# Placing units 5 to 8 of a retention layer by hand between the matmul blocks of the layer behind it

## The chip, the cores and the metric

The kernel runs on one core of one Trainium2 chip. The metric is the device time of one execution in microseconds; the median of 13 runs is compared. PE is the matrix engine (TensorE), ACT is ScalarE, DVE is VectorE, POOL is GpSimd and SP is SyncE, which only issues DMAs. Each engine has its own queue and works it off in the order in which the program wrote it. PSUM is the memory that PE writes its results into, SBUF the working memory.

## What is computed

A retention layer (attention without softmax, with a decay mask) of 8 batches, 8 heads, 576 positions and head size 64, and behind it a two-layer network on the 4608 tokens that come out:

```python
def _attn_ref(q, k, v):                       # q, k, v: (8, 8, 576, 64)
    scores = scale * np.matmul(q, k.transpose(0, 1, 3, 2))
    gamma = 1.0 - 2.0 ** (-5.0 - np.arange(H))
    Dmat = np.where(rel >= 0, gamma[:, None, None] ** rel[None, :, :], 0.0)
    return np.matmul(scores * Dmat[None], v)
...
x = attn_out.transpose(0, 2, 1, 3).reshape(B * S, H * D)    # (4608, 512)
h = x @ w_in                                                # (4608, 2048)
out = np.maximum(0.01 * h, h) @ w_out                       # (4608, 512)
```

## The kernel before

**Units.** The retention is cut into 40 units: each batch gives four of 128 positions and one of 64. Unit u goes through these helpers. `load` (L115) brings q, k and v of the unit into a ring of five buffers each (`ld`, L72), so the loads of unit u have to wait for the casts of unit u-5. `casts` (L169) makes float16 of them: k on ACT (L134), q and v with their decay tables on DVE, and from unit `NEARLY` = 11 on on POOL (L142, L162). `transposes` (L174) turns q and k on PE: four matmuls with an identity for k, ACT's copy of the result (L190), four for q, DVE's copy. From unit `NPE` = 9 on there is no PE transpose: `cast_q` issues a DMA transpose from SP instead (L150). `scores` (L196) makes the masked products inside two chunks of 64 (L204) and the unit's contribution to the running state (L214). `masks` (L221) multiplies with the triangle on DVE. `states` (L231) adds up the state on DVE, two or three instructions, and copies it to float16 (L252): on ACT below `NEARLY`, on POOL from there on. `outputs` (L294) multiplies the scores with v (L307) and the queries with the states before (L318), then ACT copies one half out of PSUM (L326) and DVE adds the other and writes `xT` (L330), the transposed input of the network.

**The network.** The tokens are cut into 18 groups of 256. `g1_blocks(g)` (L420) gives eight blocks of the first layer, each of eight matmuls (L432) and one leaky-relu on ACT (L439); they need `xT` of all units of the group and share two PSUM buffers (`hps`). `g2_blocks(g)` (L446) gives eight blocks of the second layer, each of four matmuls (L455), with a DVE copy (L465) and an output DMA from SP (L467) after the fourth and the eighth. For groups 0 and 1, `g2_wide` (L486) gives sixteen such blocks on four PSUM buffers, two of them `hps` (L500, L509, L511).

**The order.** The schedule is written out: the order of the calls is the order on every engine's queue (L82). The start (L521 to L568) is by hand. From L570 to L608 the wide blocks and those of `g1[2]` have units 5 to 8 put between them. From L609 on `run` (L475) interleaves the blocks of two groups and spreads steps over them. A step n is `steady(n)` (L378): the loads of unit n+6, `scores(n)`, `outputs(n-1)`, `casts(n+2)`, `masks(n)`, `states(n)`; the order inside depends on `NEARLY`. The steps begin with n = `NFIRST` = 7 (scores only; outputs from the next on). `NRING` = 12: loads up to unit 12 are issued from POOL at the start (L553 to L558), later ones from SP by the steps.

`tr` and `sc` are one PSUM tile for units 6 to 8 (`transposes(u, sc_pool)`, one buffer): their transposes, their scores and the states take turns in it.

Of the kernel before, what the change touches and what calls it, by code (L numbers as in the profile page):

```python
# [9 lines left out]
FP = mybir.dt.float32  # L10
# [7 lines left out]
def kernel(  # L18
# [22 lines left out]
    nc = tc.nc  # L41
    B, H, S, D = q.shape
    NT, DM = out.shape
    DFF = moe_w_in.shape[1]
    P = 128
# [3 lines left out]
    NF = DFF // P  # L49
# [48 lines left out]
    NU = len(units)  # L98
    nrows = [min(P, S - P * w) for b, w in units]
    NPE = 9  # L100
    NFIRST = 7
    NEARLY = 11
    NRING = 12
    t32 = {}
    qk16 = {}
# [1 line left out]
    qkT = {}  # L107
    s16s = {}
    st16 = {}
    carry = {}  # L110

    def half(i):
# [12 lines left out]
    def loads(u, eng):  # L125
        for x in (1, 0, 2):
            load(u, x, eng)
# [41 lines left out]
    def casts(u):  # L169
        cast_k(u)  # L170
        cast_q(u)
        cast_v(u)

    def transposes(u, pool=None):  # L174

        n = nrows[u]
        qkT[u] = b_pool.tile([P, 2, NP, P], F16, name="qkT")
        if pool is None:
            trs = [y_pool.tile([P, NP, P], F16, name="yps") for x in range(2)]
        else:  # L180
            both = pool.tile([P, 2, 2 * NP, P], F16, name="sc")
            trs = [both[:, x, 0:NP, :] for x in range(2)]
        for x in (1, 0):
            for p in range(NP):
                nc.tensor.transpose(  # L185
                    trs[x][:, p, 0:n],
                    qk16[u][0:n, x, 2 * p : 2 * p + 2, :].rearrange("t h d -> t (h d)"),
                    ident[0:n, 0:n],
                )
            (nc.scalar.copy if x else nc.vector.tensor_copy)(  # L190
                out=qkT[u][:, x, :, 0:n], in_=trs[x][:, :, 0:n]
            )
# [3 lines left out]
    def scores(u):  # L196

        nb = nrows[u] // CH
        a = sc_pool.tile([P, 2, 2, NP, CH], FP, name="sc")
        sc_tiles[u] = a  # L200
        for p in range(NP):
            for g in range(2):
                for j in range(nb):
                    nc.tensor.matmul(  # L204
                        out=a[half(j), g, 0, p, :],
                        lhsT=qkT[u][half(g), 1, p, half(j)],
                        rhs=qkT[u][half(g), 0, p, half(j)],
                        start=True, stop=True, skip_group_check=True,
                    )
        if nb == 2:  # L210
            for p in range(NP):
                for j in range(2):
                    for g in range(2):
                        nc.tensor.matmul(  # L214
                            out=a[half(g), j, 1, p, :],
                            lhsT=qk16[u][half(j), 1, 2 * p + g, :],
                            rhs=v16[u][half(j), 2 * p + g, :],
                            start=True, stop=True, skip_group_check=True,
                        )

    def masks(u):  # L221
        n = nrows[u]
        s16s[u] = a_pool.tile([P, 2, NP, CH], F16, name="s16")
        nc.vector.tensor_tensor(  # L224
            out=s16s[u][0:n],
            in0=sc_tiles[u][0:n, :, 0],
            in1=mask_sb[0:n].unsqueeze(1).unsqueeze(1).to_broadcast([n, 2, NP, CH]),
            op=MUL,
        )

    def states(u):  # L231
        b, w = units[u]
        if nrows[u] < P:
            return
        st = sc_tiles[u][:, :, 1]
        s32 = a_pool.tile([P, 2, NP, CH], FP, name="s32")
        if w == 0:
            nc.vector.tensor_copy(out=s32[:, 0], in_=st[:, 0])
        else:
            nc.vector.tensor_tensor(out=s32[:, 0], in0=st[:, 0], in1=carry[b], op=ADD)  # L240
        if w % 2 == 0:
            nc.vector.tensor_tensor(out=s32[:, 1], in0=st[:, 1], in1=s32[:, 0], op=ADD)  # L242
        else:
            tmp = a_pool.tile([P, NP, CH], FP, name="stmp")
            nc.vector.tensor_tensor(out=tmp, in0=st[:, 1], in1=s32[:, 0], op=ADD)
            nc.vector.tensor_tensor(
                out=s32[:, 1], in0=tmp,
                in1=gblk_sb.unsqueeze(2).to_broadcast([P, NP, CH]), op=MUL,
            )
        carry[b] = s32[:, 1]  # L250
        st16[u] = a_pool.tile([P, 2, NP, CH], F16, name="st16")
        (nc.scalar.copy if u < NEARLY else nc.gpsimd.tensor_copy)(out=st16[u], in_=s32)  # L252

    def st_before(u, j):
        if j:
# [38 lines left out]
    def outputs(u):  # L294


        n = nrows[u]
        nb = n // CH
        b, w = units[u]
        ot = ot_pool.tile([P, 2, 2 * NP, CH], FP, name="ot")  # L300
        own = ot[:, :, 0:NP]
        far = ot[:, :, NP : 2 * NP].rearrange("q r (s j) t -> q r s (j t)", j=2)
        for hp in range(NP):
            for h in (hp, hp + NP):
                o, c = divmod(h, NP)
                for j in range(nb):
                    nc.tensor.matmul(  # L307
                        out=own[half(o), j, c, :],
                        lhsT=v16[u][half(j), h, :],
                        rhs=s16s[u][half(j), h % 2, h // 2, :],  # L310
                        start=True, stop=True, skip_group_check=True,
                    )
        for j in range(nb):
            for s in range(2):
                for o in range(2):
                    for g in range(2):
                        p = 2 * o + s
                        nc.tensor.matmul(  # L318
                            out=far[half(o), g, s, half(j)],
                            lhsT=st_before(u, j)[half(g), p, :],  # L320
                            rhs=qkT[u][half(g), 0, p, half(j)],
                            start=True, stop=True, skip_group_check=True,
                        )
        t0 = (b * S + P * w) % XR
        tmp = a_pool.tile([P, NP, P], FP, name="own")
        nc.scalar.copy(  # L326
            out=tmp[:, :, 0:n].rearrange("q c (j t) -> q c j t", t=CH),
            in_=own[:, 0:nb].rearrange("q j c t -> q c j t"),
        )
        nc.vector.tensor_tensor(  # L330
            out=xT[:, :, t0 : t0 + n].rearrange("q (s g) t -> q g s t", g=2),
            in0=far[:, :, :, 0:n],
            in1=tmp[:, :, 0:n].rearrange("q (s g) t -> q g s t", g=2),
            op=ADD,
        )
# [41 lines left out]

    def steady(n):  # L378
        def go():
            if NRING < n + 6 < NU:  # L380
                loads(n + 6, nc.sync)
            if n < NU:
                scores(n)
            if n > NFIRST:
                outputs(n - 1)
            if n + 2 >= NEARLY:
                casts(n + 2)
            if n < NU:
                masks(n)
                states(n)  # L390
            if n + 2 < NEARLY:
                casts(n + 2)

        steps.append((n - 1, go))

# [5 lines left out]
    NG = len(sizes)  # L401
    ends = []
# [8 lines left out]
    def run_steps(upto):  # L411
        nonlocal done
        while done < upto:
            steps[done][1]()
            done += 1
# [59 lines left out]
    def run(upto, *lists):  # L475

        order = sorted(
            ((n + 0.5) / len(ls), x, n) for x, ls in enumerate(lists) for n in range(len(ls))
        )
        a = done  # L480
        for m, (_, x, n) in enumerate(order):
            lists[x][n]()
            run_steps(min(upto, a + -(-(upto - a) * (m + 1) // max(1, len(order) - 3)), done + 1))
        run_steps(upto)
# [30 lines left out]
    def blocks(g, *parts):  # L515
        for fq in parts:
            for m in (2 * fq, 2 * fq + 1):
                g1[g][m]()
# [46 lines left out]
    masks(4)  # L565
    blocks(0, 3)
    transposes(5)
    blocks(1, 3)  # L568

    wide = g2_wide([(0, 0), (0, 1), (1, 0), (1, 1)])  # L570

    def some(a, b):
        for m in range(a, b):
            wide[m]()

    some(0, 2)
    scores(5)
    outputs(4)
    masks(5)
    states(5)  # L580
    some(2, 4)
    casts(6)
    some(4, 5)
    transposes(6, sc_pool)
    some(5, 7)
    scores(6)
    outputs(5)
    masks(6)
    states(6)
    some(7, 9)  # L590
    casts(7)
    outputs(6)
    some(9, 12)
    transposes(7, sc_pool)
    casts(8)
    some(12, 15)
    run_steps(1)
    some(15, 16)
    g1[2][0]()
    transposes(8, sc_pool)  # L600
    g1[2][1]()
    g1[2][2]()
    run_steps(2)
    for m in (3, 4, 5):
        g1[2][m]()
    run_steps(3)
    for m in (6, 7):
        g1[2][m]()  # L608
    for g in range(3, NG):  # L609
        run(ends[g + 1], g1_blocks(g), g2_blocks(g - 1))  # L610
    run(ends[NG], g2_blocks(NG - 1))


# [28 lines left out]
```

## Time and profile before

| what | us |
|---|---|
| median of 13 runs | 322.99 |
| lowest and highest of the 13 | 320.57, 327.39 |
| the profiled execution | 327.39 |
| its span in the trace | 325.6 |
| PE busy | 299.7 (92%) |
| ACT, DVE, POOL busy | 139.2, 120.0, 113.2 |

The profiled execution is the longest of the 13. The 1.8 us between its time and its span lie outside the first and the last instruction. The trace holds 9255 instructions; PE's are 4042 matmuls, each with a weight load that the profile keeps as PEld. PE is busy for all of the 44 us from 267 to 311 us; where it isn't at work earlier is what the prediction looks at. "Releaser" is the instruction or DMA whose end let a waiting one go, as the profile infers it.

### The profile page before, as it was taken

The page shows a single profiled execution, that of the slowest core. Times are in us where ns is not written, and L with a number is a line of the kernel's source. Part 1 is how long each engine was busy: PE and PEld are TensorE (multiplying, and loading weights), DVE is VectorE, ACT ScalarE, POOL GpSimd, SP SyncE. Part 2 cuts the span into 40 slices and gives each one's busy share as a digit, 9 for nine tenths or more (in the row PEclk, how much of TensorE's full clock was granted, in tenths as well). Part 3 has the DMA queues.
Part 4 walks back from the last instruction along what each step waited for, and adds up shares of the span by engine and source line. Part 5 has one row for each costly group of instructions (what it writes and reads, how often), then busy time and mean ns, then how long its engine had stood idle before and what let it go on. Part 6 is the DMA issues. An engine that isn't in the chain of part 4 may idle for free.

```text
span 325.6 us, 9255 instructions
## 1 busy us (share of the span) xinstructions
PE 299.7 (92%) x4042; PEld 198.8 (61%) x4042; DVE 120.0 (37%) x226; ACT 139.2 (43%) x244; POOL 113.2 (35%) x135
## 2 busy tenths in 40 slices
PE   1769996865999999999999999999999999999995
PEld 0447853444766666666666666666666666666652
DVE  2653234374333334332342524343333263321101
ACT  3444742234644454445354545444444554333320
POOL 8847656542032515450333505350425343000000
PEclk9975999798999999999999999999999999999999
DMA  7999999994898799978686859994977241000011
GB/s 178 217 200 221 234 235 177 210 227 93 168 197 195 156 148 185 233 152 189 136 191 139 186 115 217 214 196 114 198 161 153 76 99 50 34 34 34 32 64 64
DMA packets 117863, 49.82 MB, mean 153 GB/s; under 512 B 106880, under 2 KB 110976, under 8 KB 117824
## 3 DMA queue, kind: packets, MB, share of 16 engines
q1 hardware_dynamic: 110400, 35.79, 52.9%
q0 software_dynamic: 7136, 13.37, 21.2%
q8 instruction: 31, 0.51, 0.7%
q10 hardware_dynamic: 288, 0.08, 0.1%
q14 instruction: 8, 0.07, 0.1%
HBM read 36.78 MB, written 9.44 MB: 142 GB/s over the span
## 4 chain that ended last, share of the span: by engine, by line
PE 80%; DMA 7%; DVE 5%; POOL 3%; ACT 3%; issue 1%; SPq 1%; ACTq 0%; POOLq 0%
PE hps L432 37%; PE yps L455 33%; DMA qkT<-qk 3%; DMA w_in<-in_moe_w_in_dram 3%; POOL t L120 3%; PE sc L204 3%; PE ot L318 2%; PE hps L500 1%; PE ot L307 1%; PE yps L500 1%; PE sc L214 1%; DVE s L224 1%; DVE xT L330 1%; ACT qk L134 1%; ACT own L326 1%
## 5 line engine op out<-in xcount | busy, mean ns | idle before, releaser
L432 PE MATMUL hps<-xT,w_in 128*128 128x256 f16 x1152 | 151.7, 278 | 5.1 <-ACT gt L439 3.3
L439 ACT ACTIVATE gt<-hps 128x512 f16<-128x512 f32 x144 | 85.8, 597 | 133.5 <-PE hps L432 133.2
L432 PEld LDWEIGHTS <-w_in 128*128 128x128 f16 x1152 | 114.0, 100 | 46.6 <-issue 6.1
L455 PE MATMUL yps<-w_out,gt 128*128 128x512 f16 x512 | 130.4, 380 | 0.0
L455 PEld LDWEIGHTS <-gt 128*128 128x128 f16 x512 | 47.6, 98 | 35.4
L252 POOL CAST st<-s 128x512 f16<-128x512 f32 x23 | 14.0, 611 | 139.8 <-DVE s L242 70.8
L330 DVE TENSOR_TENSOR xT<-ot,own 128x512 f16<-128x512 f32 (+1 forms) x36 | 22.8, 632 | 90.3 <-ACT own L326 90.3
L465 DVE COPY osb<-yps 128x512 f32<-128x512 f32 x32 | 22.0, 688 | 79.2 <-PE yps L455 79.2
L142 POOL TENSOR_TENSOR qk<-t,cs 128x512 f16<-128x512 f32 (+1 forms) x29 | 30.2, 1042 | 7.8 <-DMA t<-in_q_dram 4.7
L162 POOL TENSOR_TENSOR v<-t,cs 128x512 f16<-128x512 f32 (+1 forms) x29 | 30.5, 1051 | 0.9 <-PE ot L307 0.8
L224 DVE TENSOR_TENSOR s<-sc,cs 128x512 f16<-128x512 f32 (+1 forms) x40 | 27.2, 679 | 5.7 <-PE sc L214 5.1
L134 ACT CAST qk<-t 128x512 f16<-128x512 f32 (+1 forms) x40 | 24.8, 619 | 4.8 <-DMA t<-in_k_dram 4.8
L326 ACT COPY own<-ot 128x512 f32<-128x512 f32 (+1 forms) x36 | 19.4, 538 | 8.3 <-PE ot L318 7.0
L185 PEld LDWEIGHTS <-qk 128*128 128x128 f16 (+1 forms) x72 | 5.3, 112 | 17.2 <-ACT qk L134 9.1
L204 PEld LDWEIGHTS <-qkT 64*64 64x64 f16 x576 | 8.5, 110 | 10.8 <-issue 8.4
L204 PE MATMUL sc<-qkT 64*64 64x64 f16 x576 | 13.0, 202 | 1.2 <-DMA qkT<-qk 0.5
L252 ACT CAST st<-s 128x512 f16<-128x512 f32 x9 | 5.6, 618 | 19.1 <-DVE s L242 11.7
L185 PE MATMUL yps<-ident,qk 128*128 128x128 f16 (+1 forms) x48 | 5.3, 260 | 8.8 <-ACT qk L134 6.7
L120 POOL DMA_DIRECT2D t<-in_q_dram x13 | 11.3, 867 | 6.0 <-DMA w_out<-in_moe_w_out_dram 1.9
L318 PE MATMUL ot<-qkT,st 64*64 64x64 f16 x456 | 11.4, 196 | 1.6 <-ACT st L252 1.6
L120 POOL DMA_DIRECT2D t<-in_v_dram x13 | 11.1, 852 | 3.6 <-DMA w_out<-in_moe_w_out_dram 1.4
L120 POOL DMA_DIRECT2D t<-in_k_dram x12 | 10.3, 856 | 5.2 <-issue 2.2
(42 smaller groups left out, 161.1 us busy)
## 6 DMA issues: line engine op xcount, KB each, us to landing
out_dram<-osb SPq DMA_DIRECT2D x36, 256.0 KB, 2.3
t<-in_k_dram SPq DMA_DIRECT2D x22, 256.0 KB, 4.5
t<-in_q_dram SPq DMA_DIRECT2D x21, 256.0 KB, 5.1
t<-in_v_dram SPq DMA_DIRECT2D x21, 256.0 KB, 5.1
t<-in_q_dram POOLq DMA_DIRECT2D x11, 256.0 KB, 8.3
t<-in_v_dram POOLq DMA_DIRECT2D x11, 256.0 KB, 8.5
t<-in_k_dram POOLq DMA_DIRECT2D x10, 256.0 KB, 8.8
w_in<-in_moe_w_in_dram POOLq DMA_DIRECT2D x8, 256.0 KB, 10.5
```

The lines of the kernel that those rows point to most:

```text
L120: eng.dma_start(out=t[0:n], in_=(q, k, v)[x][b, :, P * w : P * w + n, :].rearrange("h t d -> t h d"),)
L134: nc.scalar.copy(out=qk16[u][0:n, 1], in_=t32[u, 1][0:n])
L142: (nc.vector if u < NEARLY else nc.gpsimd).tensor_tensor(out=t[0:n, 0], in0=t32[u, 0][0:n], in1=tab_sb[0:n, w % 2, 0, :].unsqueeze(2).to_b ...
L162: (nc.vector if u < NEARLY else nc.gpsimd).tensor_tensor(out=t[0:n], in0=t32[u, 2][0:n], in1=tab_sb[0:n, w % 2, 1, :].unsqueeze(2).to_broa ...
L204: nc.tensor.matmul(out=a[half(j), g, 0, p, :], lhsT=qkT[u][half(g), 1, p, half(j)], rhs=qkT[u][half(g), 0, p, half(j)], start=True, stop=T ...
L224: nc.vector.tensor_tensor(out=s16s[u][0:n], in0=sc_tiles[u][0:n, :, 0], in1=mask_sb[0:n].unsqueeze(1).unsqueeze(1).to_broadcast([n, 2, NP, ...
L326: nc.scalar.copy(out=tmp[:, :, 0:n].rearrange("q c (j t) -> q c j t", t=CH), in_=own[:, 0:nb].rearrange("q j c t -> q c j t"),)
L330: nc.vector.tensor_tensor(out=xT[:, :, t0 : t0 + n].rearrange("q (s g) t -> q g s t", g=2), in0=far[:, :, :, 0:n], in1=tmp[:, :, 0:n].rear ...
L432: nc.tensor.matmul(out=hps[:, f, :], lhsT=w_in16[:, c, fc * P : (fc + 1) * P], rhs=xT[:, c, t0 % XR : t0 % XR + tok], start=(c == 0), stop ...
L439: nc.scalar.activation(out=g_tiles[g][:, fb * nf : (fb + 1) * nf, :], in_=hps, func=mybir.ActivationFunctionType.Lrelu,)
L455: nc.tensor.matmul(out=y_cur[g, tb], lhsT=g_tiles[g][:, f, tb * P : (tb + 1) * P], rhs=w_out16[:, f, :], start=(f == 0), stop=(f == NF - 1),)
L465: nc.vector.tensor_copy(out=osb, in_=y_cur[g, tb])
```

## The change

- `NFIRST` and `NEARLY` become 9. Units 9 and 10 are thereby cast on POOL, and the state of unit 10 is copied on POOL.
- `transposes` issues all eight matmuls of a unit first, then ACT's and DVE's copy.
- `states` can leave its copy to `state_copy`, which is called on its own for units 7 and 8.
- Units 5 to 8 are written out by hand in another order (the diff), from the end of group 1's first layer on. The first four blocks of `g2_blocks(2)` come ahead of `run`, which starts with one list of eight and one of four blocks.
- The casts of units 9, 10 and 11, and with them their DMA transposes, are called by hand between the blocks of `g1[2]` and `g2_blocks(2)`, and the loads of unit 13 behind them.
- A step is now: `scores(n)`, `outputs(n-1)`, `casts(n+3)`, `masks(n)`, `states(n)`, loads of unit n+5.
- The last 128 tokens of the second layer are made in two column parts, 384 and 128 wide, each with a copy (DVE, then ACT) and an output DMA (SP, then ACT's queue) of its own.

```diff
-    NFIRST = 7
-    NEARLY = 11
+    NFIRST = 9
+    NEARLY = 9
...
@@ transposes
                     ident[0:n, 0:n],
                 )
+        for x in (1, 0):
             (nc.scalar.copy if x else nc.vector.tensor_copy)(
...
-    def states(u):
+    def states(u, copy=True):
...
         carry[b] = s32[:, 1]
+        st32[u] = s32
+        if copy:
+            state_copy(u)
+
+    def state_copy(u):
         st16[u] = a_pool.tile([P, 2, NP, CH], F16, name="st16")
-        (nc.scalar.copy if u < NEARLY else nc.gpsimd.tensor_copy)(out=st16[u], in_=s32)
+        (nc.scalar.copy if u < NEARLY else nc.gpsimd.tensor_copy)(out=st16[u], in_=st32[u])
...
@@ steady
-            if NRING < n + 6 < NU:
-                loads(n + 6, nc.sync)
             if n < NU:
                 scores(n)
             if n > NFIRST:
                 outputs(n - 1)
-            if n + 2 >= NEARLY:
-                casts(n + 2)
+            casts(n + 3)
             if n < NU:
                 masks(n)
                 states(n)
-            if n + 2 < NEARLY:
-                casts(n + 2)
+            if n + 5 < NU:
+                loads(n + 5, nc.sync)
...
     transposes(5)
-    blocks(1, 3)
+    g1[1][6]()
+    outputs(4)
+    g1[1][7]()
+    scores(5)
+    masks(5)
+    states(5)
...
-    some(0, 2)
-    scores(5)
-    outputs(4)
-    masks(5)
-    states(5)
-    some(2, 4)
+    some(0, 4)
+    outputs(5)
     casts(6)
-    some(4, 5)
+    some(4, 6)
     transposes(6, sc_pool)
-    some(5, 7)
+    some(6, 9)
     scores(6)
-    outputs(5)
     masks(6)
     states(6)
-    some(7, 9)
+    some(9, 12)
     casts(7)
+    some(12, 13)
     outputs(6)
-    some(9, 12)
+    some(13, 14)
     transposes(7, sc_pool)
+    some(14, 16)
+    scores(7)
+    masks(7)
+    states(7, copy=False)
+    more(g1[2], 0, 2)
+    state_copy(7)
+    more(g1[2], 2, 3)
     casts(8)
-    some(12, 15)
-    run_steps(1)
-    some(15, 16)
-    g1[2][0]()
+    more(g1[2], 3, 4)
+    outputs(7)
     transposes(8, sc_pool)
-    g1[2][1]()
-    g1[2][2]()
-    run_steps(2)
-    for m in (3, 4, 5):
-        g1[2][m]()
-    run_steps(3)
-    for m in (6, 7):
-        g1[2][m]()
-    for g in range(3, NG):
+    casts(9)
+    more(g1[2], 4, 6)
+    scores(8)
+    masks(8)
+    states(8, copy=False)
+    casts(10)
+    more(g1[2], 6, 8)
+    state_copy(8)
+    more(g2, 0, 2)
+    outputs(8)
+    casts(11)
+    loads(13, nc.sync)
+    more(g2, 2, 4)
+    run(ends[4], g1_blocks(3), g2[4:])
+    for g in range(4, NG):
         run(ends[g + 1], g1_blocks(g), g2_blocks(g - 1))
-    run(ends[NG], g2_blocks(NG - 1))
+    g2 = g2_blocks(NG - 1)
+    run(ends[NG], g2[:4])
+    y = y_pool.tile([P, DM], FP, name="yps")
+    for a, b in ((0, 3 * P), (3 * P, DM)):
+        for f in range(NF):
+            nc.tensor.matmul(
+                out=y[:, a:b],
...
+        osb = o_pool.tile([P, DM], FP, name="osb")
+        (nc.vector.tensor_copy if a == 0 else nc.scalar.copy)(out=osb[:, a:b], in_=y[:, a:b])
+        (nc.sync if a == 0 else nc.scalar).dma_start(out=out[NT - P : NT, a:b], in_=osb[:, a:b])
```

`some(a, b)` calls the wide blocks a to b-1, `more(list, a, b)` those of a list; both only call.

More of the change, by code (lines that the diff above doesn't have):

```diff
@@ L109 @@
     st16 = {}
+    st32 = {}
     carry = {}
@@ L574, in some, with more @@
             wide[m]()
-    some(0, 2)
-    scores(5)
-    outputs(4)
-    masks(5)
-    states(5)
-    some(2, 4)
+    g2 = g2_blocks(2)
+    def more(blocks, a, b):
+        for m in range(a, b):
+            blocks[m]()
+    some(0, 4)
+    outputs(5)
     casts(6)
-    some(4, 5)
+    some(4, 6)
     transposes(6, sc_pool)
-    some(5, 7)
+    some(6, 9)
     scores(6)
-    outputs(5)
     masks(6)
     states(6)
-    some(7, 9)
+    some(9, 12)
     casts(7)
+    some(12, 13)
     outputs(6)
-    some(9, 12)
+    some(13, 14)
     transposes(7, sc_pool)
+    some(14, 16)
[5 more added lines that the diff above has]
+    more(g1[2], 2, 3)
     casts(8)
-    some(12, 15)
-    run_steps(1)
-    some(15, 16)
-    g1[2][0]()
+    more(g1[2], 3, 4)
+    outputs(7)
     transposes(8, sc_pool)
-    g1[2][1]()
-    g1[2][2]()
-    run_steps(2)
-    for m in (3, 4, 5):
-        g1[2][m]()
-    run_steps(3)
-    for m in (6, 7):
-        g1[2][m]()
-    for g in range(3, NG):
-        run(ends[g + 1], g1_blocks(g), g2_blocks(g - 1))
-    run(ends[NG], g2_blocks(NG - 1))
+    casts(9)
[13 more added lines that the diff above has]
+    for g in range(4, NG):
+        run(ends[g + 1], g1_blocks(g), g2_blocks(g - 1))
+    g2 = g2_blocks(NG - 1)
[5 more added lines that the diff above has]
+                out=y[:, a:b],
+                lhsT=g_tiles[NG - 1][:, f, P : 2 * P],
+                rhs=w_out16[:, f, a:b],
+                start=(f == 0),
+                stop=(f == NF - 1),
+            )
+        osb = o_pool.tile([P, DM], FP, name="osb")
+        (nc.vector.tensor_copy if a == 0 else nc.scalar.copy)(out=osb[:, a:b], in_=y[:, a:b])
+        (nc.sync if a == 0 else nc.scalar).dma_start(out=out[NT - P : NT, a:b], in_=osb[:, a:b])
 _INS = ['q', 'k', 'v', 'moe_w_in', 'moe_w_out']
```

## The prediction

> **What bounds the kernel now.** I read the page's 40 slices first, then PE's waits, then PE's instructions in order of time.
>
> ```profile
> PE   1769996865999999999999999999999999999995
> PEclk9975999798999999999999999999999999999999
> DMA  7999999994898799978686859994977241000011
> ```
>
> A slice is 8.14 us. From slice 11 (89.5 us) on PE is full and at full clock, so from there only less PE work or an earlier start helps. Slices 6 to 10 (49 to 89 us) are not full, and two of them show a lower clock: the stretch where units 5 to 8 stand between the blocks. PE's waits of the whole kernel (us in total, times, longest) name what it waits for:
>
> ```profile
> PE yps L185 <- ACT qk L134: 6.7, 3, 4.5
> PE hps L432 <- ACT gt L439: 3.3, 1, 3.3
> PE sc L185 <- ACT qkT L190: 3.1, 3, 1.7
> PE ot L318 <- ACT st L252: 1.6, 1, 1.6
> PE sc L185 <- ACT qk L134: 0.9, 1, 0.9
> PE sc L204 <- DMA qkT<-qk: 0.5, 1, 0.5
> ```
>
> The first belongs to the start, which the change leaves. The rest lies in the stretch. In order of time (start, length; in brackets PE's idle time before it and its releaser):
>
> ```profile
> 57.30 0.26 PE L318 MATMUL ot<-qkT,st 64*64 64x64 f16 x8 [1.57 <-ACT st L252]
> 57.49 1.04 PE L500 MATMUL yps<-w_out,gt 128*128 128x512 f16 x4
> 58.36 3.46 PE L500 MATMUL hps<-w_out,gt 128*128 128x512 f16 x8
> ...
> 71.23 0.38 PE L185 MATMUL sc<-ident,qk 128*128 128x128 f16 x4 [1.71 <-ACT qkT L190]
> 71.45 2.92 PE L432 MATMUL hps<-xT,w_in 128*128 128x256 f16 x16
> ...
> 80.67 1.03 PE L432 MATMUL hps<-xT,w_in 128*128 128x256 f16 x8 [3.33 <-ACT gt L439]
> ```
>
> The reader sees two things: waits for a copy that was asked for too late, and eight matmuls in 3.46 us that take 1.89 us elsewhere.
>
> **What the Trainium skill says.** "TensorE: Matmul & The Clock Gate", Part 1, says that PE falls to half clock after about an idle window of 3.4 us and needs about as long a busy one to come back. The halving agrees (3.46 against 1.89 us); here it followed idle times of 1.57 and 1.71 us that stood close to others, so short gaps that add up are enough. The same page has ACT, DVE and POOL as strict queues, which the trace agrees with: ACT's leaky-relu at 80.03 us, long computable, waits behind the state copy (78.99) and the k cast (79.51). "DMA: Bandwidth & Descriptors", "Issuing engines are not separate DMA queues": all queues share 16 engines; the slices with DMA at 9 fit. "SBUF — State Buffer", "Who interferes with whom": a DVE operation with two inputs in SBUF and a POOL one that reads SBUF shut each other out; the trace has one v cast on DVE at 1.55 us beside a POOL cast, 0.68 elsewhere.
>
> **The change, part by part.** Prices from the trace: a first-layer block 0.87, a second-layer block 0.86, eight transposes 0.44, scores with outputs of a unit 0.56 to 0.76 by spacing (mean 0.65), DVE mask 0.68, state sums 0.8 (two) or 1.3 (three), ACT copies and casts 0.6, POOL cast 1.04, POOL state copy 0.61.
>
> *What is lost now.* From 41.27 (transposes of unit 5) to 91.53 us (end of unit 11's scores and unit 10's outputs) are 50.3 us. In it stand 14 first-layer blocks (12.2), 19 second-layer (16.3), four transposes (1.8), seven pairs of scores and outputs (4.5): 34.8. Lost: 15.5. The waits in brackets sum to 10.0 (0.87, 0.67, 0.22, 1.57, 0.67, 0.51, 0.44, 1.71, 3.33); the slow stretches cost 3.3 (3.30 for 1.72 at 58.36, 2.85 for 1.74 at 71.45, 0.6 around); the rest is refilling the array after each wait, some 0.2 each.
>
> *The new order on PE.* I went through each engine's queue by these prices. Unit 5: transposes to 41.7, block, outputs(4), block, scores(5) to 44.2; mask, sums and state copy done by 46.7; outputs(5) wanted after four blocks, at 47.7: free. Unit 6: casts follow ACT's and DVE's outputs work, k at 49.5, q at 50.3; transposes wanted at 49.9: about 0.1 late. Copies by 51.4, scores(6) wanted 53.3. State copy by 56.5, outputs(6) wanted 57.3. Unit 7: cast by 57.1, transposes at 58.7; copies 60.3, scores(7) 61.0; osb copies free `hps` by 61.8 for the second block at 62.3; state copy 64.5, outputs(7) 64.9. Unit 8: cast_k stands behind a leaky-relu and ends at 65.7 where its transposes are wanted at 65.3: 0.45 late; its scores and a block 0.15 each; state copy 71.7, outputs(8) 72.1; xT done 73.9, first block of group 3 at 74.2. The transposes without a copy between them drop the 3.1 us row. No gap comes near the 1.6 us after which the clock fell, so the 3.3 should go too. What is late next in this stretch is ACT's queue at unit 8, about 0.75 in all.
>
> *Data.* It is the same cover: loads of 5 to 12 leave POOL as before (unit 12's wait for unit 7's casts, which stay at 57), and units 7 and 8 are cast no more than 1 us earlier. POOL gets four casts more (4 x 1.04) and the copy of state 10. It is free at 61 and reaches them one after the other by 69.5. They meet DVE's casts of unit 8: up to 0.9 each, under blocks. The DMA transposes of 9 to 11 leave SP at 68, 70 and 74 instead of 70, 80 and 86, wanted at 75, 78 and 81; landing took 4.0 (median), 6.2 at most.
>
> *The new stall.* Loads of unit 13 were issued at 68.1; now they stand behind transpose 11 on SP, about 75.5. Its q lands 5.1 later, near 81.2. POOL's queue is casts(12), casts(13), state_copy(10): the copy waits for the load, two casts and itself, 83.9. PE wants it for outputs(10) at step 11, near 81.5. That is 2.5 us, with everything behind it on PE. Bounds: none if the loads land in 3.2 (shortest), 4 to 5 if they are slow. ACT's k cast of 13 has the same wait but a leaky-relu buffer covers it. Step 12 comes near 89.9, state_copy(11) 88.1: free.
>
> *Steady steps.* Loads lead their casts by two steps instead of four, DMA transposes by three instead of two. The shortest two steps are 8.4 us; SP's load issue, landing and casts fit in them, so nothing is added. The 0.5 for a DMA transpose at 202 and 0.2 of refill go: -0.7.
>
> *Tail.* The last 128 tokens' second part is 16 matmuls of 128 columns. An identity transpose of that shape takes 0.055; 16 x (0.162 + 0.055), the first an estimate from the same page's gap of columns/2.4 ns + 2.5, give 3.5 for 3.46 now: nothing. If weight loads (0.098 each) showed, +0.7. Behind it a copy of 128 columns by ACT, some 0.26 by 0.37 for 256 and 0.59 for 512, instead of DVE's 0.69, and a smaller DMA: -0.5.
>
> *Sum.* Lost after: 0.75 + 2.5, four refills of 0.2: 4.05 of 15.5. -11.4 - 0.7 - 0.5 = -12.6: 327.39 becomes 314.8, span 325.6 becomes 313.0. The profiled run is 4.4 above the median. It has 3.3 of slow clock in the stretch and 4.3 ahead of it (3.57 and 3.53 for 16 matmuls at 21.9 and 27.2, for 1.74, and small ones). If the 4.4 is slow clock in that proportion, 1.9 of my gain isn't in the median run: 322.99 - 10.7 = **312.3**.
>
> **Rivals.**
> 1. *Loads late behind POOL's queue.* Loads 13 to 16, three steps close together, come at 8 us (POOL's loads took 8.3 to 8.8 under full DMA) instead of 5: step 11 waits 5.4, step 12 1.5, step 13 1: 5.4 more than counted, 317.7. For it: DMA slices at 9, steps 3.5 us apart. Against: SP's loads never took over 6.2.
> 2. *The waits move inside the hand-placed stretch.* Margins of 0.4 to 0.9 at state copies of 6, 7, 8 and osb copies; where each of the four units waits 2 us the clock falls again and 8 + 2 come back: 322, no change.
> 3. *Slower.* The halved load lead binds in every close step. From load issue to the outputs that need the state behind it are 12.7 us at the tightest; less 3 on SP, 2.1 casts, 0.6 copy, 7.0 is left for landing. Above that about 12 close steps pay the excess: with 8.1 us 13 us, 312.3 + 13 = 325. It decides from 7.9 us on. Measured: 3.2 to 6.2.
> 4. *The copies' split does nothing*, since PE waits for the tile all the same: 3.1 and three refills come back, 316.
>
> **Numbers.** A measurement of this kernel tells some 0.5% (1.6 us) from no change. Forecast with its bounds (no POOL stall and all slow clock in the median: 308; with 4: 316): 0.68. Rival 1 with small slips and the copies: 0.16. No change (rival 2): 0.06. Slower (rival 3): 0.10. Faster 0.84. The range 308 to 318.5 leaves out rivals 2 and 3 and a few hundredths of the best and of rival 1.
>
> **What would show it.** Right: PE at 9 in slices 6 to 10 but for one; clock at 9 there; no "sc L185 <- ACT qkT L190"; scores(9) at about 75 instead of 81.6; one wait of outputs(10) on POOL's state copy, 2 to 3 us, behind a cast that waited for unit 13's q. Wrong: DMA or ACT waits in hand-placed units (2), waits of outputs on "POOL st" in many steps (3), a landing of loads over 7 us.

## The result and the profile after

| | before | after |
|---|---|---|
| median, us | 323.28 (48 runs) | 310.81 (11 runs) |
| profiled execution, us | 327.39 | 314.17 |
| its span, us | 325.6 | 312.1 |
| transposes of unit 5 start at, us | 41.27 | 40.03 |
| from there to the end of the span, us | 284.3 | 272.1 |

The ratio after to before is 0.9619 (95% interval 0.9592 to 0.9645): 12.5 us less in the median, where 10.7 were forecast (312.3; range 308 to 318.5). The ratio is formed without the executions that lie more than 1.5% above the fastest of their kernel; both profiled ones are among these, so their times are longer than the medians. The last row leaves out the start and gives 12.2 us.

The slices of the changed kernel's page, 7.80 us each:

```profile
PE   1659999999899999999999999999999999999995
PEclk9998999999999999999999999999999999999999
```

The hole in slices 6 to 10 is gone but for one 8, and so are the slices of low clock there. The six largest of PE's waits in the whole kernel (us in total, times, longest):

```profile
PE yps L186 <- ACT qk L135: 6.9, 3, 4.8
PE yps L186 <- DVE qk L143: 2.7, 3, 1.8
PE hps L436 <- DMA w_in<-in_moe_w_in_dram: 1.9, 1, 1.9
PE ot L325 <- POOL st L259: 0.9, 1, 0.9
PE ot L325 <- ACT st L259: 0.7, 1, 0.7
PE yps L638 <- DVE osb L646: 0.6, 1, 0.6
```

The first three belong to the start, before unit 5. The 3.1 us row on ACT's copy of `qkT` and the 3.3 us row on ACT's leaky-relu have no successor. Three new or remaining waits are left, and each is told below: outputs(10) for POOL's state copy, outputs(8) for ACT's state copy, and one in the last block, which the change itself brought. In order of time on PE (start, length; idle time and releaser in brackets):

```profile
71.37 0.26 PE L325 MATMUL ot<-qkT,st 64*64 64x64 f16 x8 [0.71 <-ACT st L259]
71.56 1.90 PE L459 MATMUL yps<-w_out,gt 128*128 128x512 f16 x8
...
74.27 0.31 PE L206 MATMUL sc<-qkT 64*64 64x64 f16 x8
...
82.02 0.26 PE L325 MATMUL ot<-qkT,st 64*64 64x64 f16 x8 [0.87 <-POOL st L259]
```

Eight matmuls of 512 columns take 1.90 us throughout: the 3.46 us of before are gone. The scores of unit 9 run at 74.27 us instead of 81.64.

### The profile page after: what moved, and what is told of

It is laid out like the page before. It is cut to its first block, busy times and chain, and to the rows that moved or that the text cites. A ratio compares the mean times of both kernels' runs of the same rounds, so it can differ in the third digit from the quotient of the medians.

```text
span 312.1 us, 9261 instructions
## 1 busy us (share of the span) xinstructions
PE 293.9 (94%) x4058; PEld 197.2 (63%) x4058; DVE 121.3 (39%) x222; ACT 138.5 (44%) x244; POOL 119.3 (38%) x140
## 4 chain that ended last, share of the span: by engine, by line
PE 87%; DMA 5%; POOL 4%; DVE 1%; ACT 1%; issue 1%; POOLq 0%
PE hps L436 39%; PE yps L459 34%; DMA w_in<-in_moe_w_in_dram 4%; POOL t L121 3%; PE sc L206 3%; PE yps L504 2%; PE hps L504 2%; PE ot L325 2%; DMA t<-in_q_dram 1%; PE ot L314 1%; PE yps L638 1%; PE sc L216 1%; DVE s L248 1%; PE sc L186 1%; ACT st L259 0%
## 5 line engine op out<-in xcount | busy, mean ns | idle before, releaser
L436 PE MATMUL hps<-xT,w_in 128*128 128x256 f16 x1152 | 147.7, 274 | 1.9 <-DMA w_in<-in_moe_w_in_dram 1.9
L436 PEld LDWEIGHTS <-w_in 128*128 128x128 f16 x1152 | 112.6, 98 | 40.9 <-issue 2.4
L459 PE MATMUL yps<-w_out,gt 128*128 128x512 f16 x496 | 126.7, 380 | 0.0
L459 PEld LDWEIGHTS <-gt 128*128 128x128 f16 x496 | 45.9, 98 | 33.9
L469 DVE COPY osb<-yps 128x512 f32<-128x512 f32 x31 | 21.3, 688 | 73.1 <-PE yps L459 73.1
L143 POOL TENSOR_TENSOR qk<-t,cs 128x512 f16<-128x512 f32 (+1 forms) x31 | 32.5, 1050 | 39.7 <-DMA t<-in_q_dram 32.5
L259 POOL CAST st<-s 128x512 f16<-128x512 f32 x24 | 14.7, 610 | 85.5 <-DVE s L244 44.6
L163 POOL TENSOR_TENSOR v<-t,cs 128x512 f16<-128x512 f32 (+1 forms) x31 | 33.0, 1064 | 2.4 <-DMA t<-in_v_dram 1.8
L143 DVE TENSOR_TENSOR qk<-t,cs 128x512 f16<-128x512 f32 (+1 forms) x9 | 6.9, 768 | 12.1 <-DMA t<-in_q_dram 12.1
```

Of the source, the lines that this page charges most:

```text
L143: (nc.vector if u < NEARLY else nc.gpsimd).tensor_tensor(out=t[0:n, 0], in0=t32[u, 0][0:n], in1=tab_sb[0:n, w % 2, 0, :].unsqueeze(2).to_b ...
L163: (nc.vector if u < NEARLY else nc.gpsimd).tensor_tensor(out=t[0:n], in0=t32[u, 2][0:n], in1=tab_sb[0:n, w % 2, 1, :].unsqueeze(2).to_broa ...
L436: nc.tensor.matmul(out=hps[:, f, :], lhsT=w_in16[:, c, fc * P : (fc + 1) * P], rhs=xT[:, c, t0 % XR : t0 % XR + tok], start=(c == 0), stop ...
L459: nc.tensor.matmul(out=y_cur[g, tb], lhsT=g_tiles[g][:, f, tb * P : (tb + 1) * P], rhs=w_out16[:, f, :], start=(f == 0), stop=(f == NF - 1),)
L469: nc.vector.tensor_copy(out=osb, in_=y_cur[g, tb])
```

## The experiments

Theory A, from the prediction: the gain is PE's waits in the hand-placed stretch, and what is left there are two queues, POOL's and ACT's, and a tail that gains 0.5. The rivals: the gain sits in one other part of the change (the split of the transposes, the casts moved to POOL, the steps' new order); the halved lead of the loads is the danger. "Ratio" is always to the kernel before, with its 95% interval; these intervals are 0.4 to 2.1% wide, so for effects around 1 us the trace decides and the time only goes along. "From unit 5 to the end" is the stretch of the table's last row, in the profile of the run.

### The changed kernel again

> The changed kernel once more, as the base of the three runs beside it. Both theories: 310.8 us, ratio to before 0.962. In its trace I look for the same three losses: outputs(8) waiting 0.7 us for the state copy of unit 8, outputs(10) waiting 0.9 us for POOL's state copy, and 0.65 us between the two parts of the last block.

311.46 us, ratio 0.963 (0.9595 to 0.9666). From the transposes of unit 5 to the end: 272.1 us, as in the first profile. The wait for POOL is 1.46 us in this execution, that of outputs(8) is missing, the gap in the last block is 0.65 us again. So two of the three losses vary from one execution to the next; the third doesn't.

### The last block in two PSUM tiles

```diff
-    y = y_pool.tile([P, DM], FP, name="yps")
     for a, b in ((0, 3 * P), (3 * P, DM)):
+        y = y_pool.tile([P, DM], FP, name="yps")
```

> The changed kernel with a PSUM tile of its own for each of the two column parts of the last block. Theory A (the 128-column part waits because both parts share one tile that DVE is still copying): the 0.65 us gap goes and the time falls by 0.6 to 0.8 us. Theory B (the tail is set by the output DMA's landing): the gap goes, the end stays, 0 us.

First the end of the kernel before (its last 16 matmuls start at about 318.2 us), then that of the changed one:

```profile
313.89 7.93 PE L455 MATMUL yps<-w_out,gt 128*128 128x512 f16 x36
...
304.71 2.76 PE L638 MATMUL yps<-w_out,gt 128*128 128x384 f16 x16
...
307.51 0.56 DVE L646 COPY osb<-yps 128x384 f32<-128x384 f32 x1 [1.91 <-PE yps L638]
...
308.12 1.05 PE L638 MATMUL yps<-w_out,gt 128*128 128x128 f16 x16 [0.65 <-DVE osb L646]
...
309.21 0.27 ACT L646 COPY osb<-yps 128x128 f32<-128x128 f32 x1 [8.02 <-PE yps L638]
```

Then that of this run:

```profile
304.78 3.66 PE L638 MATMUL yps<-w_out,gt 128*128 128x384 f16 x32
...
307.58 0.56 DVE L646 COPY osb<-yps 128x384 f32<-128x384 f32 x1 [1.91 <-PE yps L638]
...
308.47 0.27 ACT L646 COPY osb<-yps 128x128 f32<-128x128 f32 x1 [7.21 <-PE yps L638]
```

With one tile the second part waits until DVE has read the first. With two, PE runs through (32 matmuls in 3.66 us). From the first matmul of the block to the end of the span it is 311.4 - 304.78 = 6.6 us here and 312.1 - 304.71 = 7.4 in the changed kernel. The kernel before has 7.4 too (from 318.2, which is 20 matmuls at 0.216 us behind 313.89, to 325.6). So the change's split of the last block gains nothing, and with a tile for each part 0.8. 310.85 us, ratio 0.9605 (0.9566 to 0.9644): theory A, though the time alone wouldn't tell it.

### The loads of unit 13 earlier

```diff
     transposes(8, sc_pool)
+    loads(13, nc.sync)
     casts(9)
...
     casts(11)
-    loads(13, nc.sync)
```

> The changed kernel with the loads of unit 13 issued ahead of casts(9), not behind casts(11). Theory A (POOL's queue: the state copy of unit 10 stands behind casts(13), which wait for that load): outputs(10) no longer waits, 0.9 us and a refill of 0.2 less: -1.0 us. Theory B (outputs(10) waits for something else, or DMA transposes 9 to 11 are pushed back by the loads in front of them): the wait stays or scores(9) waits, 0 or slower by up to 2 us.

313.14 us, ratio 0.9674 (0.9636 to 0.9712). The interval overlaps that of the changed kernel, but from unit 5 to the end it is 275.1 us against 272.1: slower. Its waits of PE have no POOL row, as A said, but a new one:

```profile
PE sc L206 <- DMA qkT<-qk: 2.9, 1, 2.9
```

SP's queue shows what that transpose stood behind:

```profile
60.59 0.39 SPq L121 DMA_DIRECT2D t<-in_k_dram  x1
61.17 2.56 SPq L121 DMA_DIRECT2D t<-in_q_dram  x1
63.90 4.86 SPq L121 DMA_DIRECT2D t<-in_v_dram  x1
68.92 4.78 SPq L151 DMA_TRANSPOSE qkT<-qk  x3
```

Two issues whose median is 0.6 and 0.9 us in the changed kernel held SP for 2.6 and 4.9 us, and the DMA transpose of unit 9 behind them left at 68.92 us; in after_again, whose unit 5 comes 0.7 us later, it left at 63.15. POOL's last loads were still landing at that time (8.5 to 8.9 us each), and q and v of unit 13 took 9.9 and 8.4 us to land. That the one held up the other was not tested: single issues of up to 2.7 us stand in the changed kernel too, where POOL has no load under way. The reason for the wait at step 11 was right, the remedy cost more. So I put the loads one transpose further back:

```diff
     casts(10)
+    loads(13, nc.sync)
     more(g1[2], 6, 8)
...
     casts(11)
-    loads(13, nc.sync)
```

> The changed kernel with the loads of unit 13 between the DMA transposes of units 10 and 11: later than in loads13_early, where two of them sat 2.6 and 4.9 us on SP and pushed transpose 9 back by 6 us. Theory A: transposes 9 and 10 leave as in the changed kernel, transpose 11 has some 7 us to spare, and outputs(10) doesn't wait for POOL: -1.0 us. Rival (SP's queue blocks there as well): scores(10) or (11) wait for their transposes, 0 or slower.

310.69 us, ratio 0.9586 (0.9539 to 0.9632). Its PE has no wait on POOL and none on a DMA transpose. From unit 5 to the end 270.3 us against 272.1. A holds here, by the trace; the intervals overlap.

### The state copy of unit 8 on POOL

```diff
-        (nc.scalar.copy if u < NEARLY else nc.gpsimd.tensor_copy)(out=st16[u], in_=st32[u])
+        (nc.scalar.copy if u < NEARLY - 1 else nc.gpsimd.tensor_copy)(out=st16[u], in_=st32[u])
...
+    state_copy(8)
     more(g1[2], 6, 8)
-    state_copy(8)
```

> The changed kernel with the state copy of unit 8 on POOL, in its queue between casts(10) and casts(11). Theory A (DVE's last state product of unit 8 took 2.32 us instead of 0.42 because POOL's casts of units 11 and 12 held the shared reads): POOL now waits for that product instead of running against it, it is back near 0.4 us, outputs(8) no longer waits: -0.9 us. Theory B (the product is slow for another reason): it stays at 2.3 us, outputs(8) waits as before or longer, 0 to +0.5 us.

The product in question, on DVE, in the first profile of the changed kernel, where outputs(8) waited 0.71 us, and one of POOL's casts beside it:

```profile
67.89 0.42 DVE L247 TENSOR_TENSOR stmp<-sc,s 128x256 f32<-128x256 f32 x1
68.35 2.32 DVE L248 TENSOR_TENSOR s<-stmp,cs 128x256 f32<-128x256 f32 x1
69.35 1.03 POOL L143 TENSOR_TENSOR qk<-t,cs 128x512 f16<-128x512 f32 x1
```

In after_again it takes 0.70, and outputs(8) doesn't wait. In this run it takes 0.53:

```profile
65.17 0.53 DVE L248 TENSOR_TENSOR s<-stmp,cs 128x256 f32<-128x256 f32 x1
```

311.41 us, ratio 0.9631 (0.9583 to 0.9679), no different from the 0.963 beside it. That two SBUF inputs on DVE and POOL's casts shut each other out is what the Trainium skill says ("SBUF — State Buffer", "Who interferes with whom"); the trace agrees in place (POOL's casts run without a gap from 62.6 to 71.6 us), and the operation before it, with one input in PSUM, keeps its 0.42.

More telling is where the product ends: in all nine profiles in which it takes over 0.42 us, that is 0.28 or 0.29 us after a cast on POOL ends (here at 70.67, after 70.38). So it waits for POOL's casts, for one of them as a rule, for two or three in a row in three profiles: 2.32 here, 2.92 in tail_two_tiles, where outputs(8) waited 1.31 us, and 1.72 in loads13_mid, without a wait behind it. With the edit POOL's next instruction waits for the product, so it can no longer lose to the casts of units 11 and 12; the two profiles with the edit (0.53, and 0.42 in all_three) agree. A is right on the cause; what the edit is worth, the time doesn't tell.

### One part alone, one part undone

```diff
# split_only: the kernel before with this; no_split: the changed kernel without it
                     ident[0:n, 0:n],
                 )
+        for x in (1, 0):
             (nc.scalar.copy if x else nc.vector.tensor_copy)(
```

> The kernel before with one part of the change: all eight transposes of a unit ahead of both copies. Theory A (the placement of units 5 to 8 is what pays): the 3.1 us row of waits on the k copy goes, some of it comes back at the next wait: 1.5 to 3.5 us faster than before, about 320.5. Rival (the split is the main part): 6 us or more.

> The changed kernel with ACT's copy of k put back between the two sets of four transposes. Theory A: units 6, 7 and 8 wait some 0.7 us each for that copy and refill 0.2: 2 to 2.7 us slower than the changed kernel, 313 to 313.5. Rival (PE doesn't wait there any more in the new order, or the split is the main part): 0, or over 5 us slower.

split_only: 320.9 us, ratio 0.9923 (0.9903 to 0.9944), 2.5 us faster. no_split: 313.41 us, ratio 0.9723 (0.9658 to 0.9788), 2 to 3 us slower than the changed kernel, with the row back:

```profile
PE sc L186 <- ACT qkT L191: 2.4, 3, 1.1
```

Both as A said. In split_only the wait of the sixth block of `g1[2]` on ACT's leaky-relu is still there (3.65 us), and that on the state copy of unit 6 (1.57): those are the placement's.

```diff
# nearly11
-    NEARLY = 9
+    NEARLY = 11
```

> The changed kernel with NEARLY back at 11: casts of units 9 and 10 on DVE, state copies of 9 and 10 on ACT. Theory A (moving these casts to POOL is no source of the gain): outputs(10) no longer waits for POOL (-1.0), DVE has 2.7 us more in front of the masks and states of unit 8 (0 to +1): between -1 and +0.5 us against the changed kernel. Rival (the move to POOL is a main part): 2 to 4 us slower.

310.03 us, ratio 0.9629 (0.9543 to 0.9715): the casts' move to POOL is no source of the gain. I had one point wrong: the wait on POOL stays (0.9 us), since now the state copy of unit 11 stands behind a cast.

```diff
# short_lead
-            if n + 5 < NU:
-                loads(n + 5, nc.sync)
+            if n + 4 < NU:
+                loads(n + 4, nc.sync)
...
-    loads(13, nc.sync)
```

> The changed kernel with steady loads one step later still: unit n+4 at step n, and unit 13 by step 9. This is the mechanism of the slower rival, brought on: the state copy on POOL stands behind casts(n+3), which wait for loads issued one step before. Theory A (the lead of two steps was just enough, by 2 us at the tightest): now short by about 2 us in the close steps, waits of outputs on the POOL state copy in ten or more steps, 6 to 25 us slower than the changed kernel. Rival (the lead doesn't matter, loads land long before): under 1 us slower.

336.13 us (332.79 to 343.35), ratio 1.0378 (1.0275 to 1.0482): some 25 us slower than the changed kernel. PE's largest wait:

```profile
PE ot L325 <- POOL st L259: 15.0, 7, 4.3
```

Seven waits, not ten, but up to 4.3 us each, and the clock is lower (0.955 on average in this execution, the slowest of the four). Two more waits of PE, 2.3 and 2.2 us, stand at unit 8, ahead of anything this edit touches on PE, DVE or POOL: DVE's casts of q and v took 5.02 and 3.52 us beside POOL's casts of units 9 to 12, where they take 0.68 alone. In the other profiles with this order they took 0.7 to 1.5 us; the prediction had priced the collision at up to 0.9 each, under blocks. So the changed kernel itself can lose time there in some executions. The mechanism of the slower rival exists, and is dear. With a lead of two steps the changed kernel stays on the right side of it, by one step.

### The new order of units 5 to 8 without the rest

```diff
# old_steady: the changed kernel with this
     def go():
+            if n + 6 < NU:
+                loads(n + 6, nc.sync)
             if n < NU:
                 scores(n)
             if n > NFIRST:
                 outputs(n - 1)
-            casts(n + 3)
+            casts(n + 2)
             if n < NU:
                 masks(n)
                 states(n)
-            if n + 5 < NU:
-                loads(n + 5, nc.sync)
...
-    casts(11)
     loads(13, nc.sync)
+    loads(14, nc.sync)
# placement_only: also NEARLY = 11, the k copy between the transposes, the last block in one piece
```

> The changed kernel with the steps' order of before: loads of n+6 first, casts of n+2; units 13 and 14 loaded by hand. Theory A: the step order is worth the 0.7 us of a DMA transpose that came late at 202 us, against the POOL wait of step 11, which goes; so -0.5 to +1.5 us against the changed kernel, with one or more waits of scores on a DMA transpose in the trace. Rival (the third step of lead for the transposes is a main part of the gain): 3 to 6 us slower.

> The new order of units 5 to 8 with the other parts of the change undone: copy of k between the transposes, NEARLY 11, the last block in one piece, steps as before (casts of n+2, loads of n+6 at their head; units 13 and 14 loaded by hand to fit). Theory A (placement pays by itself): 313 to 315 us, 9 to 10 faster than the kernel before. Rival (it pays only with the steps' new order or the split, each of which alone gives 2 to 3): 318 or more.

old_steady: 318.32 us, ratio 0.9851 (0.9796 to 0.9906), 7 us slower than the changed kernel. placement_only: 321.57 us, ratio 0.9943 (0.9917 to 0.9968), only 2 us faster than the kernel before. Here my theory falls short: I had put the early DMA transposes and the steps' order at 1 us or so, and the placement alone at 9 to 10. The trace of old_steady, PE:

```profile
74.55 0.32 PE L206 MATMUL sc<-qkT 64*64 64x64 f16 x16
...
83.49 0.43 PE L206 MATMUL sc<-qkT 64*64 64x64 f16 x16 [5.59 <-DMA qkT<-qk]
...
86.17 3.43 PE L436 MATMUL hps<-xT,w_in 128*128 128x256 f16 x16
```

and its SP:

```profile
69.45 0.70 SPq L121 DMA_DIRECT2D t<-in_v_dram  x1
70.25 2.55 SPq L121 DMA_DIRECT2D t<-in_k_dram  x1
...
76.25 1.58 SPq L121 DMA_DIRECT2D t<-in_v_dram  x1
78.00 2.02 SPq L151 DMA_TRANSPOSE qkT<-qk  x1
```

PE comes through the hand-placed stretch without a wait, exactly as placed, and reaches the scores of unit 11 at 77.9 us. Their DMA transpose leaves SP at 78.0, behind the loads of units 13, 14 and 15, and PE waits 5.6 us for it; then 16 matmuls take 3.43 us instead of 1.91 at the lowered clock. That makes up the 7. In placement_only it is 6.3 us, plus the 2.4 of the k copies. In the changed kernel that same transpose is the last of three that SP works off from 66.0 us on; it leaves at 72.9, ahead of the loads:

```profile
66.00 8.14 SPq L151 DMA_TRANSPOSE qkT<-qk  x3
74.25 0.51 SPq L121 DMA_DIRECT2D t<-in_k_dram  x1
```

So the placement is worth little without the transposes issued ahead: it takes PE's own waits away, and they keep the DMA from taking their place. The reverse, transposes ahead with units 5 to 8 as before, wasn't run. That the loads of three units stood in front of transpose 11 is in part my edit's doing (13 and 14 by hand, 15 by step 9). How much would be left with the old steps and only that transpose ahead wasn't run and stays open.

### All that helped, together

loads13_mid, the two tiles and the state copy of unit 8 on POOL in one kernel.

> loads13_mid with a PSUM tile for each part of the last block and unit 8's state copy on POOL. Theory A, if the parts add: -0.8 for the tail, -1.0 for step 11, 0 to -0.9 for unit 8 (that collision isn't in every run): 308 to 309.2 us. Rival (unit 8's copy on POOL pushes casts(11) and transpose 11 back and step 11 waits): no better than tail_two_tiles, 310.8.

309.02 us, ratio 0.9566 (0.9524 to 0.9608). From unit 5 to the end 269.2 us: 1.1 less than loads13_mid, 2.8 less than the changed kernel (272.1). In the trace PE has no wait left from unit 5 to the end; its last one is before the first block of the first layer, at 21 us. It beats both kernels; against the changed one the intervals still overlap by a hair, so that part rests on the trace.

## Why the prediction was right, step by step

- **The lost time.** 15.5 us were counted as lost between unit 5's transposes and unit 10's outputs, 4.05 as left. Measured: from 40.03 to 82.20 us is 42.2, with three second-layer blocks and one first-layer block more in it, so 34.8 + 3.5 of work: 3.9 left. Right, and the slow clock went with the waits as said. How long a gap has to be for that these runs don't tell: in the kernel before the clock fell after a wait of 1.57 us and not after the one of 3.33 (24 matmuls in 2.93 us from 82.13); in split_only it did not fall after the same wait of 1.57 (eight of 512 columns in 1.89) and fell after 3.65; in st8_on_pool it stayed at 1.00 after 1.58.
- **What it is made of.** Not right in the parts. The wait for unit 8's k cast (0.75 in all) isn't among PE's waits: I had added ACT's durations (0.6), but queued ACT instructions start 0.47 to 0.52 us apart in this trace. In its place outputs(8) waited 0.71 for its state, because of the DVE product above: I had priced that collision for the casts of unit 8 and called it covered, and not looked at the next DVE instruction of the kind. And scores and outputs that stand apart take 0.48 + 0.47 (unit 5 after) where a pair takes 0.76 (unit 11 before), which I had left out: those of this stretch take some 6.5 us without their waits, not 4.5. That the total still comes within 0.2 us is luck: these two errors stand against the k cast and a stall 1.6 us smaller than forecast (next point).
- **The new stall.** The chain was as predicted: load 13 behind transpose 11, casts(13), state copy, outputs(10). On POOL:

```profile
79.36 1.04 POOL L143 TENSOR_TENSOR qk<-t,cs 128x512 f16<-128x512 f32 x1 [7.79 <-DMA t<-in_q_dram]
80.36 1.04 POOL L163 TENSOR_TENSOR v<-t,cs 128x512 f16<-128x512 f32 x1
81.35 0.61 POOL L259 CAST st<-s 128x512 f16<-128x512 f32 x1
```

  Its size was too large: 2.5 forecast, 0.6 to 1.6 measured over the five executions that have this order (0.87 above), because q landed in 4.4 us (74.93 to 79.36) and PE came to it 0.9 later than worked out.
- **Steady steps.** PE is busy for 160.0 of the 160 us from 140 to 300, no wait for a DMA transpose is left. Right. The slower rival's bound (7.0 us for a landing) was not reached, though not by much: 6.7 us at most for the loads from 70 us on. short_lead shows what lies behind it.
- **Tail.** -0.5 forecast, 0 measured. The step that failed: I took the second part as running right behind the first, and both share one tile. With two it is -0.8, and PE's 32 matmuls take 3.66 us where I had estimated 3.5.
- **The median.** The sum, -12.6, was made against the profiled run; from unit 5 on it measures -12.2, in the medians -12.5. I then took 1.9 off, because the profiled run's 4.4 us above its median might be slow clock inside the stretch. That was the one step that moved the forecast away from the result: as far as one profile of the kernel before tells, the excess lies in the start. Unit 5's transposes came at 41.27 us in that run, with a mean granted clock of 0.86 up to 36 us. Of the thirteen profiles of the other kernels, the six with a clock of 1.00 there have them at 36.2 to 37.0, the seven with 0.91 to 0.95 at 38.0 to 40.0.
- **Data.** That the DMA transposes of 9 to 11 leave SP earlier (68, 70 and 74, wanted at 75, 78 and 81) stood in the prediction as a margin only. old_steady shows how much hangs on it: with the old steps 7 of the 12.5 us come back, in part through the loads that the edit itself puts in front. The forecast of the whole came out since the change held both parts; its account of which part pays did not.

## What to carry to other kernels

When waits of the bounding engine are taken out of a stretch, everything that feeds the next stretch is wanted earlier by as much: list the DMAs there with the time at which they leave their queue, and move them in the same edit. In an in-order queue a copy that somebody waits for mustn't stand behind an instruction that waits for a load. Splitting a last block only overlaps if its parts have buffers of their own.

## What was not expected of the hardware

An issue of a load on SP, 0.6 to 0.9 us in the median, took 2.6 and 4.9 us in loads13_early, so a load can be dear for what is queued behind it. Queued ACT copies of 0.6 us follow each other at about 0.5: for a chain through ACT the distance of starts counts, not the sum of durations. And a DVE instruction with two inputs in SBUF can lose to several POOL casts in a row: 2.92 us for a product of 0.42 (tail_two_tiles), 5.02 for a cast of 0.68 (short_lead).
